# Four interleaved attention layers: a new table of slots, maxima that lead by 14 steps, accumulator copies on VectorE at a layer's end

## The chip, the cores and the metric

The kernel runs on one core of a Trainium2 chip. The metric is the time of one execution on the device, in microseconds; the kernel before is given as the median of three runs. A core has TensorE (PE, matrix products into eight PSUM banks of 128 x 512 fp32), VectorE (DVE), ScalarE (ACT), GpSimd (POOL) and SyncE (SP), which here issues all transfers. PE runs a weight load (PEld) and a matmul for each product.

## The reference, cut to what matters

Four layers run one after the other on x of 2048 rows and 576 columns, with 32 heads of 18 columns. Layers 0 and 2 ("A") have keys and values of their own for each head, layers 1 and 3 ("B") share one key and one value head.

```
x = x + _A_ref(_layernorm(x), A_wqkv, A_wo)
x = x + _B_ref(_layernorm(x), B_wq, B_wk, B_wv, B_wo)
x = x + _A_ref(_layernorm(x), A_wqkv, A_wo)
x = x + _B_ref(_layernorm(x), B_wq, B_wk, B_wv, B_wo)

scores = einsum("bhqd,bhkd->bhqk", q, k) * (Dh ** -0.5)
p = softmax(scores, axis=-1)
o = einsum("bhqk,bhkd->bhqd", p, v)
```

The softmax subtracts each row's maximum, so that the scores are computed twice: once for the maxima and once for the exponentials.

## The kernel before, in words

A layer has three parts: the projections (with the maxima of the first units woven between their matmuls), the attention, and the output projection. The order of every engine is the order in which the program is written; no scheduler moves anything, and each engine takes its instructions in that order.

**Units.** Two heads (a = 0, 1, a pair p) and 512 queries (u) make a unit; a layer has 64 units, w = 0 to 63. A unit needs 32 "e" products (L734: 64 rows by 512 queries; their exponentials are taken by ACT in L738 and written to `pt`), 32 tests for maxima and 4096 columns of "PV" (L759: the value product, 128 x 19 weights in four column groups, accumulated in the one bank `oacc`). Three kinds of product serve the maxima: "m" (L586, reduced by DVE in L593), "d" (L579, a difference of key blocks, of which ACT takes the positive part into `r`, L583) and "t" (an m whose reduction by DVE, L590, adds that `r`). Head a uses rows 64a to 64a+63 of PE, so that a pair of letters in the table below runs side by side.

**The table.** `UNIT` (L65) is the written order of a unit: each two-letter word is a pair, its first letter for head 0 and its second for head 1, and the number behind it is how many PV columns follow. Words up to a number are called a stretch here; the table has twelve. `LAST` (L67) is the table of the units that have no maxima left. PV lags the exponentials by `LAG` columns, and is cut where it passes a multiple of 512 columns, since a step's four `pt` tiles go together (`pv_cols`, L742). When a unit's PV is complete, `oacc` is copied to `oc` by ACT (L765), and the next PV may start only behind that copy.

**Maxima.** They lead the exponentials by `LEAD` steps; a unit has 8 steps of four e. With LEAD 16 the unit w of the table carries the maxima of unit w + 2, and the 32 pairs of maxima that come before the first unit are woven into the projections: `woven(max_pair, left, every)` (L273) puts one pair of m behind each `every` projection matmuls. `run_todo` (L833) issues at a given step what `at` has put down for it.

**Behind a unit's last maximum** DVE forms `neg` (L710), POOL splits it into `hl` (L713, L714), DVE transposes (L719), SP stores `m_d` (L721) and loads it back as two rows of the operand `big` (L725); the unit's exponentials need these rows. **Behind a unit's PV** POOL makes `os` out of `oc` (L772 by the helper line L179, then L773), SP loads `lt` (L778), POOL forms the reciprocal (L782), and so on to `o_d`.

**Buffers.** The e and d products share four PSUM banks (tag "e"), the m and t products have three (tag "m"); `oacc` is the eighth. The SBUF tiles `pt`, `r`, `oc` and those of the projections share 15 buffers (tag "p", L173): a new tile takes a buffer that is free in the written order, and its writer waits until the last reader of the old tile is done.

**Weights of the next layer** are loaded in the last units: `load(...)` puts a transfer into `raw`, and `finish_loads` (L212) splits what has arrived on POOL, which waits for the transfer there.

Of the kernel before, what the change touches and what calls it, by code (L numbers as in the profile page):

```python
# [10 lines left out]
AF = mybir.ActivationFunctionType  # L11
# [9 lines left out]
NPAIR = H // 2  # L21
# [21 lines left out]


STEPS = 8
LEAD = 16
NM_AT = 2
ROW_AT = 5
SUM_AT = 3
# [12 lines left out]

UNIT = """ee md 384 me me em 512 dm md em 320 me ee em 192 em me 384 et ee mm 384 me ee em 384 dm me em 384  # L65
          em me 256 me te ee 256 em em 384 et te me 256"""
LAST = "ee ee 512 " * 8  # L67
LAG = 896


def slots(text):
# [9 lines left out]
UNIT, LAST = slots(UNIT), slots(LAST)  # L81
# [4 lines left out]
def max_ops(kinds):  # L86
    pairs = kinds.count("d")
    rest = [(qc, kb) for qc in range(4) for kb in range(4) if qc >= pairs or kb > 1]
    seen, ops = {"d": 0, "t": 0}, []
    for k in kinds:  # L90
        if k == "m":
            ops.append((k, *rest.pop(0)))
        else:
            ops.append((k, seen[k], 0))
            seen[k] += 1
    assert not rest
    return ops


MAX_OPS = [max_ops(k) for k in KINDS]  # L100
PLAIN = [(i // 2 % 4, i // 8 % 2 * 2 + i % 2) for i in range(16)]
FIRST_SHARED = 3

# [2 lines left out]
def tile_kernel(ctx: ExitStack, tc: tile.TileContext, A_x, A_wqkv, A_wo, B_x, B_wq, B_wk, B_wv, B_wo, out):  # L106
    nc = tc.nc
# [67 lines left out]
    def copy(eng, dst, src):  # L175
        if eng is nc.scalar:
            eng.activation(dst, src, AF.Copy)
        else:
            eng.tensor_scalar(dst, src, 1.0, 0.0, op0=OP.mult, op1=OP.add)  # L179
# [93 lines left out]
    def woven(f, left, every):  # L273
        assert not weave["left"]
        weave.update(f=f, left=left, every=every, n=0)
# [119 lines left out]
    for layer in range(4):  # L395
# [159 lines left out]
        def max_mm(a, tile):  # L555

            n = m_next[a]
            w, i = divmod(n, 16)
            shared = w >= FIRST_SHARED
            kind = "m"  # L560
            if n < len(m_first):
                w, qc, kb = m_first[n]
            elif shared:
                kind, qc, kb = MAX_OPS[a][i]
            else:
                qc, kb = PLAIN[i]
            p, u = divmod(w, 4)
            q, k = ops(p)
            if (p, u) not in mxs:
                mxs[p, u] = mxd[w % 2] if shared else pool.tile([P, 32], F32, name="mx")  # L570
            mx = mxs[p, u]
            b = 64 * a
            c0 = u * 512 + qc * P
            r0 = 16 * a + 4 * qc + kb
            m_next[a] += 1
            m_done[0] += 1
            if kind == "d":
                ps = etile("psd")
                nc.tensor.matmul(ps, q[b:b + 3 * DH, c0:c0 + P], kds[p % 2 if is_a else 0][b:b + 3 * DH],  # L579
                                 start=True, stop=True)  # L580
                r = ptile("r")
                diffs[a].append(r)
                nc.scalar.activation(r, ps, AF.Relu)  # L583
            else:
                ps = tile("psm")
                nc.tensor.matmul(ps, q[b:b + KM, c0:c0 + P], k[b:b + KM, kb * 512:(kb + 1) * 512],  # L586
                                 start=True, stop=True)
                if kind == "t":
                    r = diffs[a].pop(0)
                    nc.vector.tensor_tensor_reduce(out=r, in0=ps, in1=r, scale=1.0, scalar=-3.0e38, op0=OP.add,  # L590
                                                   op1=OP.max, accum_out=mx[:, r0:r0 + 1])
                else:
                    nc.vector.reduce_max(mx[:, r0:r0 + 1], ps, axis=AX.X)  # L593
            m_count[p, u] = m_count.get((p, u), 0) + 1
            if m_count[p, u] == 32:
                max_final(p, u)

        def max_pair():
            if is_a and m_done[0] % 4 == 0:
                run_todo(m_done[0] // 4)  # L600
            for a in range(2):
                max_mm(a, etile if a else mtile)
            if not is_a and m_done[0] == 46:
                max_store(0, 0)
            elif not is_a and m_done[0] == 54:
                max_rows(0, 0)
# [53 lines left out]
        for T in range(4):  # L660
            if T == 0 and not is_a:
                fixed_rows(k_slot(0), True)
                fixed_rows(q_slot(0), False)
            if is_a:
                ts = range(0 if T or layer else 2, 9) if T < 3 else (6, 7, 8, 0, 4)
            else:
                ts = (4, 0, 1, 2, 3) if T < 3 else (4, 0, 1)
            for i, t in enumerate(ts):
                if not is_a and T == 2 and i == 1:
                    woven(max_pair, 12, 4)  # L670
                elif not is_a and T == 3:
                    woven(max_pair, *((3, 4), (4, 3), (4, 3))[i])
                project(T, t, not is_a and T >= 2)
                if is_a and T == 3 and i == 2:
                    load_k(0, 0, 1536)
                    load_q(0, 0, 512)
                    last_values()

                if T < 3 and (i % 2 != (T + layer == 0) if is_a else i < 4):
                    advance()  # L680
                if T == 0 and is_a and i < 6:
                    finish_loads(*((2,), (4,))[i] if layer == 0 and i < 2 else ())
                    if i < 4:
                        for c in (0, 1) if i == 0 else (i + 1,):
                            load_wsm(c, A_wqkv[:, 2 * D:])
                    if layer == 0 and i < 3:
                        load_x(5 + i)
                if not is_a and i < 2:
                    (load_q if i else load_k)(0, T * 512, T * 512 + 512)
                if vts and i != 0:  # L690
                    v_trans(*vts.pop())
            if is_a and T < 2:
                for c in range(4 * T, 4 * T + 4):
                    for h, ps in enumerate(project_v(c)):
                        nc.scalar.activation(v_dst(c)[:, h], ps, AF.Copy)
# [55 lines left out]
        def pv_block(n, c0, c1):  # L751

            p, u, i = *divmod(n // STEPS, 4), n % STEPS * 4
            cs = slice(c0, c1)
            turn[0] += 1
            for i in range(i, i + 4) if turn[0] % 2 else range(i + 3, i - 1, -1):
                a, kc = (i // 2) % 2, i // 4 * 2 + i % 2
                j = 64 * a + 32 * (kc % 2)
                nc.tensor.matmul(oacc[j:j + DH + 1, cs], v_of(kc)[:, 2 * p + a if is_a else 0, :], pts[p, u, i][:, cs],  # L759
                                 start=kc < 2 and c0 == 0, stop=kc >= 14 and c1 == 512)  # L760
                if c1 == 512:
                    pts.pop((p, u, i))
            if c1 == 512 and i // 4 == STEPS - 1:
                oc = ocs[p, u] = ptile("oc")
                nc.scalar.activation(oc, oacc, AF.Copy)  # L765


        def o_sum(p, u):
# [35 lines left out]
        def at(b, f, *args):  # L804
            todo.setdefault(b, []).append((f, args))
# [16 lines left out]
        for c in range(5):  # L822
            at(49 + 4 * c, finish_loads)
            at(48 + 4 * c, load_wsm, c, A_wo if is_a else B_wo, nc.gpsimd, nc.gpsimd, True)
            if layer < 3:
                b = LEAD + 32 * (NPAIR - 1) + 2 * c
                load = load_b if is_a else load_a
                at(b - 29, finish_loads)
                at(b + 3, finish_loads)
                at(b - 30, load, c, (2,), nc.gpsimd, nc.gpsimd, True)  # L830
                at(b + 2, load, c, (0,), nc.gpsimd, nc.gpsimd, True)

# [14 lines left out]
        late, n_e = LAG, 0  # L847
        for w in range(4 * NPAIR):
            p, u = divmod(w, 4)
            more_m = m_done[0] < 4 * ns  # L850
            e_next = [0, 0]
            for kinds, cols in UNIT if more_m else LAST:
                run_todo(LEAD + STEPS * w + sum(e_next) // 4)
                for a in range(2):
                    if kinds[a] == "e":
                        n = e_next[a]
                        e_next[a] += 1
                        exp_mm(p, u, n // 2 * 4 + 2 * a + n % 2, mtile if not more_m and n_e % 7 % 2 else etile)
                        n_e += 1
                    else:  # L860
                        max_mm(a, mtile)
                skip = min(late, cols)
                late -= skip
                pv_cols(cols - skip)
            assert e_next == [16, 16]
# [40 lines left out]
```

## Time and profile before

| | us |
|---|---|
| median of 3 runs (5727.47 to 5728.47) | 5728.04 |
| the profiled execution | 5728.76 |
| its span, first to last instruction | 5727.0 |
| PE busy | 5670.4 (99%) |
| DVE busy | 4936.5 (86%) |
| ACT busy | 4915.4 (86%) |
| POOL busy | 1744.0 (30%) |
| 16 DMA engines | 17.6% on the main queue |

The three large groups of PE are the m products (L586, 7216 matmuls), the e products (L734, 8192) and PV (L759, 30784 in the records, since each fp32 product of the program is two of them). ACT is mostly the 8192 exponentials of L738 (633 ns each, overlapping), DVE mostly the 6240 maxima of L593 (682 to 685 ns, overlapping). A row of the timeline is: start us, length us, engine, line, operation, output and inputs, form, count, and in brackets the engine's idle time ahead and what ended it. Ends of matmuls are modelled, so starts are what is read.

### The profile page before, as it was taken

What the parts mean: (1) busy time and instruction counts of PE and PEld (TensorE: products, weight loads), DVE (VectorE), ACT (ScalarE), POOL (GpSimd) and SP (SyncE); (2) the same over time, 40 slices, a digit from 0 to 9 for tenths busy, and PEclk for the clock granted to TensorE, in tenths of its full rate; (3) what the DMA queues carried; (4) which work ended last, traced back from release to release, by engine and by line L of the source; (5) the groups of instructions that cost most, each with busy time, mean ns of one, the idle gap of its engine ahead of it and who ended that gap; (6) DMA issues with size and microseconds to landing.
All of it is one profiled execution on the core that took longest, in us unless ns stands there. A gap on an engine that the chain in (4) does not pass through costs nothing.

```text
span 5727.0 us, 136567 instructions
## 1 busy us (share of the span) xinstructions
PE 5670.4 (99%) x51804; PEld 2876.1 (50%) x51804; DVE 4936.5 (86%) x9505; ACT 4915.4 (86%) x9876; POOL 1744.0 (30%) x2236
## 2 busy tenths in 40 slices
PE   9999999999999999999999999999999999999999
PEld 7644444444844444444585444444447444444446
DVE  4699999997689999999647999999976999999994
ACT  2499999999279999999725999999992899999995
POOL 3143333334123333333321333333332333333332
PEclk9999999999999999999999999999999999999999
DMA  6311111111320000100253111111113201010002
GB/s 227 107 48 36 39 35 38 39 35 27 123 65 23 24 23 20 24 23 24 60 187 95 49 38 35 39 38 36 37 39 120 58 23 23 20 24 23 20 17 78
DMA packets 258555, 291.48 MB, mean 51 GB/s; under 512 B 132700, under 2 KB 172892, under 8 KB 248176
## 3 DMA queue, kind: packets, MB, share of 16 engines
q1 hardware_dynamic: 257896, 282.75, 17.6%
q8 instruction: 407, 6.67, 0.5%
q14 instruction: 252, 2.06, 0.1%
HBM read 158.77 MB, written 119.86 MB: 49 GB/s over the span
## 4 chain that ended last, share of the span: by engine, by line
PE 96%; issue 1%; ACT 1%; POOL 1%; DMA 1%; DVE 1%; SPq 0%; ACTq 0%; POOLq 0%; DVEq 0%
PE oacc L759 37%; PE pse L734 22%; PE psm L586 20%; PE psn L257 6%; PE psq L414 6%; PE psd L579 4%; ACT pt L738 1%; PE ps L249 0%; POOL ev L429 0%; DVE mx L593 0%; DMA raw<-in_B_wk_dram 0%; DMA raw<-in_A_wqkv_dram 0%; DMA big<-qk_d 0%; SPq L191 0%; PE oacc L250 0%
## 5 line engine op out<-in xcount | busy, mean ns | idle before, releaser
L738 ACT ACTIVATE pt<-pse 128x512 f32<-128x512 f32 x8192 | 4202.5, 633 | 122.6 <-PE pse L734 53.2
L593 DVE TENSOR_REDUCE mxd<-psm 128x1 f32<-128x512 f32 x5856 | 3689.7, 682 | 115.9 <-PE psm L586 52.6
L586 PE MATMUL psm<-big 62*128 62x512 f32 x7216 | 2629.2, 450 | 10.3 <-DMA big<-qk_d 6.4
L734 PE MATMUL pse<-big 64*128 64x512 f32 x8192 | 2427.9, 439 | 1.8 <-ACT evr L428 1.6
L759 PE MATMUL oacc<-pt,vbuf 128*19 128x384 f32 (+5 forms) x23584 | 1789.0, 396 | 20.7 <-ACT oc L765 17.3
L734 PEld LDWEIGHTS pse<-big 64*128 64x128 f32 x8192 | 1231.5, 185 | 925.3 <-ACT pt L738 689.8
L586 PEld LDWEIGHTS psm<-big 62*128 62x128 f32 x7216 | 1188.9, 184 | 644.6 <-DVE mxd L593 255.8
L759 PEld LDWEIGHTS oacc<-pt,vbuf 128*19 128x19 f32 x23584 | 459.8, 97 | 687.6 <-issue 572.4
L590 DVE CUSTOM_DVE_ANT_0 r<-psm,r 128x512 f32<-128x512 f32 x976 | 652.7, 688 | 140.3 <-PE psm L586 118.3
L179 POOL TENSOR_SCALAR hl<-neg 128x8 fp32r<-128x8 f32 x256 | 50.6, 198 | 1813.6 <-DVE neg L710 1813.6
L759 PE MATMUL oacc<-pt,vy 128*19 128x128 f32 (+2 forms) x7200 | 593.4, 414 | 1.2
L583 ACT ACTIVATE r<-psd 128x512 f32<-128x512 f32 x976 | 581.8, 625 | 0.6 <-PE psd L579 0.6
L795 POOL TENSOR_TENSOR os<-os,rb 96x512 f32<-96x512 f32 x256 | 327.6, 1280 | 718.1 <-DMA rb<-r_d 714.3
L179 POOL TENSOR_SCALAR os<-oc 32x512 f32<-32x512 f32 x512 | 313.6, 612 | 676.1 <-issue 560.2
L782 POOL TENSOR_TENSOR rl<-lt,mone 128x8 f32<-128x8 f32 x256 | 422.2, 1649 | 97.5 <-DMA lt<-os 94.5
L579 PE MATMUL psd<-xx,big 54*128 54x512 f32 x976 | 402.9, 452 | 0.0
L422 ACT ACTIVATE ev<-psq 128x512 fp32r<-128x512 f32 (+1 forms) x112 | 66.9, 597 | 351.5 <-PE psq L414 278.8
L773 POOL TENSOR_TENSOR os<-os,oc 96x512 f32<-96x512 f32 x256 | 327.6, 1280 | 21.3
L257 PE MATMUL psn<-wsm,xx 128*128 128x288 f32 x2240 | 316.4, 298 | 2.1 <-ACT vy L497 2.0
L257 PEld LDWEIGHTS psn<-wsm,xx 128*128 128x128 f32 x2240 | 299.7, 188 | 21.0 <-issue 17.0
L593 DVE TENSOR_REDUCE mx<-psm 128x1 f32<-128x512 f32 x384 | 244.1, 685 | 56.6 <-PE psm L586 49.7
L579 PEld LDWEIGHTS psd<-xx,big 54*128 54x128 f32 x976 | 162.0, 184 | 258.5 <-ACT pt L738 207.2
(82 smaller groups left out, 2261.3 us busy)
## 6 DMA issues: line engine op xcount, KB each, us to landing
big<-qk_d SPq DMA_DIRECT2D x180, 432.0 KB
qk_d<-ev SPq DMA_DIRECT2D x96, 512.0 KB
qk_d<-ev SPq DMA_DIRECT2D x120, 256.0 KB
rb<-r_d SPq DMA_DIRECT2D x512, 36.0 KB
o_d<-os SPq DMA_DIRECT2D x512, 36.0 KB
m_d<-tr SPq DMA_DIRECT2D x1024, 2.0 KB
o<-o_d SPq DMA_DIRECT2D x64, 256.0 KB
big<-m_d SPq DMA_DIRECT2D x512, 4.0 KB
```

Source lines behind the costliest of these rows:

```text
L179: eng.tensor_scalar(dst, src, 1.0, 0.0, op0=OP.mult, op1=OP.add)
L257: nc.tensor.matmul(ps, lhs[:, xc, :], wsm[:, wc, h * 288:(h + 1) * 288], start=i == 0, stop=i == len(TERMS) - 1)
L414: nc.tensor.matmul(ps[:n].rearrange("p (u t) -> p u t", u=2)[:, us], w[:, wc, :n], xts[T][:, us, xc, :], start=(xc, wc) == TERMS[0], stop= ...
L579: nc.tensor.matmul(ps, q[b:b + 3 * DH, c0:c0 + P], kds[p % 2 if is_a else 0][b:b + 3 * DH], start=True, stop=True)
L583: nc.scalar.activation(r, ps, AF.Relu)
L586: nc.tensor.matmul(ps, q[b:b + KM, c0:c0 + P], k[b:b + KM, kb * 512:(kb + 1) * 512], start=True, stop=True)
L590: nc.vector.tensor_tensor_reduce(out=r, in0=ps, in1=r, scale=1.0, scalar=-3.0e38, op0=OP.add, op1=OP.max, accum_out=mx[:, r0:r0 + 1])
L593: nc.vector.reduce_max(mx[:, r0:r0 + 1], ps, axis=AX.X)
L734: nc.tensor.matmul(e, k[r:r + KE, kc * P:(kc + 1) * P], q[r:r + KE, u * 512:(u + 1) * 512], start=True, stop=True)
L738: nc.scalar.activation(pt, e, AF.Exp, scale=SCALE)
L759: nc.tensor.matmul(oacc[j:j + DH + 1, cs], v_of(kc)[:, 2 * p + a if is_a else 0, :], pts[p, u, i][:, cs], start=kc < 2 and c0 == 0, stop=k ...
L782: nc.gpsimd.tensor_tensor(rl, lts.pop((p, u)), mone, op=OP.pow)
```

## The change

- `LEAD` is 14: 28 pairs of maxima lie before the first unit in place of 32, and unit w of the table carries in its first eight words the last quarter of the maxima of unit w + 1, and behind them the first three quarters of unit w + 2 (`CUT`, `MAX_OPS`).
- `UNIT` is another order of the same counts: 32 e, 4 d, 4 t, 24 m and 4096 PV columns, in twelve stretches. `LAG` is 960.
- Unit 62, before a `LAST` unit, now takes `ENDS`: the first eight words of `UNIT`, then e alone. Unit 63 keeps `LAST`.
- `max_pair` takes an "e" bank for one maximum in four in place of one in two, and the weaving in the B layers is 10 pairs behind every 5 matmuls, 2 behind every 7, 4 behind every 3 twice (before: 12 behind every 4, 3 behind every 4, and the same two).
- Once a layer has no maxima left, `oc` is copied by DVE (units 61, 62 and 63).
- The splits of the next layer's weights stand two steps later, and one at a time.

```diff
-LEAD = 16
+LEAD = 14
...
-UNIT = """ee md 384 me me em 512 dm md em 320 me ee em 192 em me 384 et ee mm 384 me ee em 384 dm me em 384
-          em me 256 me te ee 256 em em 384 et te me 256"""
+UNIT = """md ee me 256 mm ee et 384 te em 320 me me ee 320 me em 384 em em md 448 ee em dt 448 me em em 384
+          em te 256 me em ee 384 mm de me 384 me em 128"""
 LAST = "ee ee 512 " * 8
-LAG = 896
+LAG = 960
+
+CUT = 4
...
-MAX_OPS = [max_ops(k) for k in KINDS]
+ENDS = UNIT[:8] + LAST[:10] + [["ee", 0], ["ee", 4096 - 5 * 512 - sum(n for _, n in UNIT[:8])]]
+assert [[w[a] for w, _ in UNIT[:8]].count("e") for a in range(2)] == [8 - CUT] * 2
+MAX_OPS = [max_ops(k[CUT:] + k[:CUT]) for k in KINDS]
...
             for a in range(2):
-                max_mm(a, etile if a else mtile)
+                max_mm(a, etile if m_done[0] % 4 == 3 else mtile)
...
                 if not is_a and T == 2 and i == 1:
-                    woven(max_pair, 12, 4)
+                    woven(max_pair, 10, 5)
                 elif not is_a and T == 3:
-                    woven(max_pair, *((3, 4), (4, 3), (4, 3))[i])
+                    woven(max_pair, *((2, 7), (4, 3), (4, 3))[i])
...
                 oc = ocs[p, u] = ptile("oc")
-                nc.scalar.activation(oc, oacc, AF.Copy)
+                copy(nc.scalar if m_done[0] < 4 * ns else nc.vector, oc, oacc)
...
-                at(b - 29, finish_loads)
-                at(b + 3, finish_loads)
+                at(b - 27, finish_loads, 1)
+                at(b + 5, finish_loads, 1)
...
-            more_m = m_done[0] < 4 * ns
+            more_m = w < 4 * NPAIR - 2
             e_next = [0, 0]
-            for kinds, cols in UNIT if more_m else LAST:
+            for kinds, cols in UNIT if more_m else ENDS if w == 4 * NPAIR - 2 else LAST:
...
-                        exp_mm(p, u, n // 2 * 4 + 2 * a + n % 2, mtile if not more_m and n_e % 7 % 2 else etile)
+                        exp_mm(p, u, n // 2 * 4 + 2 * a + n % 2, mtile if m_done[0] == 4 * ns and n_e % 7 % 2 else etile)
```

## The prediction

> **What bounds the kernel now.** I read the page first, then the busy time by stretches, then the timeline of one unit, since a unit repeats some 250 times.
>
> ```profile
> span 5727.0 us, 136567 instructions
> PE 5670.4 (99%) x51804; PEld 2876.1 (50%) x51804; DVE 4936.5 (86%) x9505; ACT 4915.4 (86%) x9876; POOL 1744.0 (30%) x2236
> ...
> L738 ACT ACTIVATE pt<-pse 128x512 f32<-128x512 f32 x8192 | 4202.5, 633 | 122.6 <-PE pse L734 53.2
> ```
> ```profile
> sum 378.00, PE 378.00 PEld 171.60 DVE 356.28 ACT 371.38 POOL 115.63; mean PE 18.90 PEld 8.58 DVE 17.81 ACT 18.57 POOL 5.78
> ```
> ```profile
> L765 ACT ACTIVATE oc<-oacc x43: 597/597/602, 404.9 to 1194.0; 128x512 f32<-128x512 f32 x43
> ```
>
> The second fence sums twenty stretches of 18.9 us from 400 us on: PE, ACT and DVE are all nearly full. The third holds one `oc` copy per unit: 42 units in 789.1 us, so a unit takes 18.79 us. A "busy" PE may be waiting, so its floor must be read from starts:
>
> ```profile
> 403.77 1.05 PE L759 MATMUL oacc<-pt,vy 128*19 128x512 f32 x8
> 404.76 0.50 PE L579 MATMUL psd<-xx,big 54*128 54x512 f32 x1
> ...
> 405.80 0.73 PE L759 MATMUL oacc<-pt,vbuf 128*19 128x320 f32 x8
> ...
> 410.30 0.85 PE L759 MATMUL oacc<-pt,vbuf 128*19 128x128 f32 x16
> 411.08 0.49 PE L586 MATMUL psm<-big 62*128 62x512 f32 x1
> ...
> 412.81 0.50 PE L579 MATMUL psd<-xx,big 54*128 54x512 f32 x1
> ...
> 413.71 0.84 PE L759 MATMUL oacc<-pt,vbuf 128*19 128x384 f32 x8
> ...
> 414.49 0.50 PE L734 MATMUL pse<-big 64*128 64x512 f32 x1
> ...
> 415.15 0.63 PE L759 MATMUL oacc<-pt,vy 128*19 128x256 f32 x8
> 415.71 0.49 PE L586 MATMUL psm<-big 62*128 62x512 f32 x1
> ```
>
> Three pairs take 0.90 us (412.81 to 413.71), two take 0.66 (414.49 to 415.15); 256 PV columns take 0.56 and 512 take 0.99, so 1.68 ns a column and 0.13 for the switch. Both tables have eight stretches of three pairs, four of two and 4096 columns: 7.20 + 2.64 + 12 x 0.13 + 6.88 = 18.28 us. The unit of before loses 18.79 - 18.28 = 0.51 us to waits; the worst is 404.76 to 405.80, 1.04 in place of 0.90. The change can gain that 0.51 at most in a unit, or lose more.
>
> **The change part by part: the table.** Its counts of e, d, m, t are those of before, so only waits can differ. I find four terms.
>
> (1) Small pieces. With `LAG` 960 PV starts a unit at column 64 of a block. Walking the table past the multiples of 512 gives five pieces of 64 columns: one each in the stretches of 448 (the second), 256 (the second) and 384 ("me em ee"), two in the last, of 128. Before, no piece is below 128.
>
> ```profile
> L759 PEld LDWEIGHTS oacc<-pt,vbuf x23584: 94/98/157, 233.8 to 5670.0; 128*19 128x19 f32 x200
> ```
>
> A piece is two rounds of four products side by side. A round of 128 columns streams 128 x 0.84 = 107 ns, just above the 98 ns that its four weights (loaded side by side during the round before) take; so the split of 384 into two pieces costs nothing (410.30 to 411.08, as 413.71 to 414.49). A round of 64 streams 54 ns and must wait for weights: about 109 ns from start to start. The 55 ns are lost seven times (a piece that ends a stretch loses one round, the one that begins a stretch two, the pair of 64 three): 0.39 us a unit. Bounds: 0 and ten rounds, 0.55. The Trainium skill ("TensorE: Matmul & The Clock Gate", LDWEIGHTS) gives a weight load as its columns over 1.2 ns, 16 ns for 19 columns; by it the pieces would cost nothing and the sum below would fall by 95 us. The trace disagrees: 94 is the shortest of 23584.
>
> (2) Banks. A product needs one of four e banks. An exponential starts 0.54 us behind its product's place in a stretch (0.00, 0.24, 0.47 for the three pairs; 0.50 of matmul), frees its bank 0.64 later (633 ns), and the next follows after 0.48. In "md ee me 256 | mm ee et" the first stretch puts four on an idle ACT: starts 0.54, 1.01, 1.49, 1.97. The third e of the next stretch needs the third's bank, free at 2.13, and its place is 0.90 + 0.56 + 0.47 = 1.93: 0.20 us lost. "me em 384" behind "me me ee" loses 0.03. Bounds of this term: 0, and 0.51, all that before loses. The maxima are spread more evenly than before (2 or 3 in each stretch, never 3 twice in a row, where before has 1, 3, 3), and the same walk finds no wait on DVE.
>
> (3) The buffer of `oc`.
>
> ```profile
> 402.51 0.19 DVE L710 TENSOR_REDUCE neg<-mxd 128x8 f32<-128x32 f32 x1
> ...
> 402.78 0.20 POOL L179 TENSOR_SCALAR hl<-neg 128x8 fp32r<-128x8 f32 x1 [6.41 <-DVE neg L710]
> ...
> 403.06 0.20 POOL L714 TENSOR_TENSOR hl<-neg,hl 128x8 fp32r<-128x8 f32 x1
> ...
> 404.90 0.60 ACT L765 ACTIVATE oc<-oacc 128x512 f32<-128x512 f32 x1
> ...
> 405.39 1.08 ACT L583 ACTIVATE r<-psd 128x512 f32<-128x512 f32 x2
> 405.64 1.30 POOL L179 TENSOR_SCALAR os<-oc 32x512 f32<-32x512 f32 x2 [2.38 <-issue]
> ...
> 406.34 7.37 ACT L738 ACTIVATE pt<-pse 128x512 f32<-128x512 f32 x14
> ...
> 407.02 1.28 POOL L773 TENSOR_TENSOR os<-os,oc 96x512 f32<-96x512 f32 x1
> ```
>
> POOL ends its sum 3.40 us behind the start of `oc` (408.30 - 404.90), and only then is `oc`'s buffer free. In the written order the ninth ACT operation behind `oc` takes that buffer before, two `r` and six `pt` ahead of it: it would start some 4.5 us behind `oc`, a margin of 1.1. That this wait binds when POOL is late, the trace shows once:
>
> ```profile
> 1312.15 1.26 POOL L773 TENSOR_TENSOR os<-os,oc 96x512 f32<-96x512 f32 x1
> ...
> 1313.45 2.07 ACT L738 ACTIVATE pt<-pse 128x512 f32<-128x512 f32 x4 [2.03 <-POOL os L773]
> 1314.10 0.14 PEld L759 LDWEIGHTS oacc<-pt,vbuf 128*19 128x19 f32 x8 [1.82 <-ACT pt L738]
> ```
>
> In the new order only six `pt` stand between, and the first e of "em em md 448" takes the buffer: 0.49 + 6 x 0.48 = 3.4 us behind `oc`, margin 0. And the last maximum of a unit now falls into the third stretch, whose PV ends the unit: counted from the table's start the four maxima and sums of stretches two and three occupy DVE from 2.01 to 5.22, `neg` ends at 5.4, when `oc` ends too. POOL's `hl` pair (0.56 from `neg`'s end to its own, 402.70 to 403.26), written first, holds the `os` copies back by 0.4. So ACT waits 0.3 to 0.5 us in each unit, all exponentials behind it queue, and the third and fourth e/d of "ee em dt" find their banks late: PE loses 0.2 to 0.4; I take 0.30. Bounds: 0 (POOL in time), and 0.5, all of ACT's wait.
>
> (4) `max_store`, `max_rows` come two steps later relative to the exponentials. The rows leave SP behind `lt`, which waits for POOL's sum: about 10 us into a unit of 19, so 8 us are left before they are read. I cost it at nothing; if a landing took over 8 us, each unit would wait for it.
>
> A unit so takes 18.28 + 0.39 + 0.23 + 0.30 = 19.20, 0.41 more than before; full units from the second to the 62nd are 61 in a layer, 244 in all: +100 us.
>
> **The ends of the layers.**
>
> ```profile
> 1400.26 1.08 PE L734 MATMUL pse<-big 64*128 64x512 f32 x4
> ...
> 1405.46 0.42 PE L759 MATMUL oacc<-pt,vbuf 128*19 128x128 f32 x8 [1.69 <-ACT oc L765]
> ...
> 1423.60 0.63 PE L759 MATMUL oacc<-pt,vbuf 128*19 128x128 f32 x8 [2.55 <-ACT oc L765]
> ```
> ```profile
> 1409.13 13.92 ACT L738 ACTIVATE pt<-pse 128x512 f32<-128x512 f32 x28 [0.73 <-PE pse L734]
> ...
> 1427.73 9.91 ACT L738 ACTIVATE pt<-pse 128x512 f32<-128x512 f32 x20 [0.68 <-PE pse L734]
> ```
>
> The last two units run from 1400.26 to the last exponential at 1437.64: 37.4 us. PE waits twice for `oc`, which stands behind up to seven exponentials in ACT's queue, and ACT starves after it. With DVE copying (it has no maxima left; some 0.6 us each, as on ACT) unit 62 takes three stretches (4.7 us with term 2) and then 56 exponentials at 0.49 (13.92 for 28): 0.5 + 4.7 + 27.4 = 32.6. That is -4.8 in this layer; I take -17 for four. If PE went on waiting for the copies, nothing would come.
>
> Four pairs fewer lie in each layer's projections:
>
> ```profile
> 184.80 0.93 PE L257 MATMUL psn<-wsm,xx 128*128 128x288 f32 x5
> 185.66 0.50 PE L586 MATMUL psm<-big 62*128 62x512 f32 x2
> 186.09 0.93 PE L257 MATMUL psn<-wsm,xx 128*128 128x288 f32 x5
> ```
> ```profile
> 1445.70 29.90 PE psn L257 x224
> ```
>
> A pair costs 1.29 - 5 x 0.133 = 0.63 us there (its maxima are covered by DVE at 1.25 a pair); sixteen are -10 us. They reappear in unit 62, already counted. In layers 1 and 3 the weaving puts the pair that needs the last keys some 5 us later:
>
> ```profile
> 1584.16 1.46 PE L586 MATMUL psm<-big 62*128 62x512 f32 x2 [3.11 <-DMA big<-qk_d]
> ```
> ```profile
> 1585.00:1590.00 5.00, 5.00 (x13) 2.69 (x14) 1.92 (x4) 1.09 (x2) 1.27 (x1) 0.50 0.29 108
> ```
>
> That wait of 3.1 us, and the half clock behind it (0.50), which stretches the next 7 us by some 3.4, go: -13 for both layers. Against it, the first maxima rows of a B layer now leave five pairs closer to the first exponential: 0 to 3 us each, +3 in all. The later splits remove what made POOL late at 1312, here and once in layer 2: -5. The e banks that `max_pair` leaves free and the longer run without PV in the first unit I cost at nothing, within 3 us a layer either way. Sum of the ends: -17 - 10 - 13 + 3 - 5 = -42 us (0 to -60).
>
> **Sum.** Against the profiled execution, 5728.76 (0.7 above the median shown): +100 - 42 gives 5787 us.
>
> **The rivals.** *POOL is in time* (the other side): if `neg` ends 0.4 us sooner than I find, term 3 is gone. A unit takes 18.90, +27 us; with the ends 5714, faster. It decides at POOL's sum ending within 3.4 us of `oc`'s start. For it: the margin without `hl` is 0; against it: a DVE which falls behind makes `neg` later, not sooner. *The pieces are free*: term 1 is gone, 244 x 0.39 = 95 us, 5692; against it the 98 ns. *More small waits*: before's unit loses 0.51, of which the two largest, 0.14 and 0.08, are what a walk of banks finds; if 0.25 of such waits lies on top here too, 5787 + 61 = 5848. *Both the first two*: 5787 - 73 - 95, about 5620.
>
> **How the numbers follow.** The forecast 0.50 (own range 5755 to 5820, by terms 2 and 3 and the ends), POOL in time 0.20, free pieces 0.08, more waits 0.20, both 0.02. The range 5700 to 5870 leaves out the free pieces and the tails, under 2 in 10. A measurement of this kernel can tell about 0.2% (11 us) from no change. Faster by more: 0.12 of the 0.20, 0.08 and 0.02, 0.22; within: 0.06; slower: 0.72.
>
> **What would show it.** The distance of `oc` copies in mid-layer: 19.2 us (18.9 if POOL is in time). ACT waiting for `os` L773 once in each unit, 0.3 to 0.5. PV pieces of 64 columns whose rounds start 109 ns apart. At a layer's end no wait of PE for `oc` above 1 us, and no half clock between 1400 and 1430. No wait of 3 us for `big` in layer 1. The prediction is wrong if units are below 18.8, or if a new wait that I cost at nothing, the maxima rows above all, binds in each unit.

## The result: 0.7% slower, and the profile after

| | before | after |
|---|---|---|
| median, us | 5727.76 (4 runs) | 5767.66 (5766.65 to 5769.43, 4 runs) |
| ratio, 95% interval | | 1.007 (1.0053 to 1.0088) |
| span of the profiled execution, us | 5727.0 | 5765.8 |

The forecast was 5787 us in a range of 5700 to 5870. The sum is near, but two of its terms are not: one price was wrong by nearly its whole size, and others made up for it. The page of the kernel after, its head and the row of the exponentials:

```profile
span 5765.8 us, 151755 instructions
...
PE 5733.0 (99%) x59516; PEld 3007.5 (52%) x59516; DVE 4918.9 (85%) x9517; ACT 4927.5 (85%) x9864; POOL 1741.8 (30%) x2236
...
L742 ACT ACTIVATE pt<-pse 128x512 f32<-128x512 f32 x8192 | 4252.7, 632 | 185.1 <-POOL os L777 99.9
```

The waits of ACT (us in total, times, longest), and the copies of `oc` from 404 to 1194 us (durations in ns, first and last start):

```profile
ACT pt L742 <- POOL os L777: 99.9, 240, 0.5
```
```profile
L181 ACT ACTIVATE oc<-oacc x42: 624/632/645, 404.6 to 1191.4; 128x512 f32<-128x512 f32 x42
```

ACT's idle time ahead of the exponentials has a new main releaser, POOL's sum `os`, in 240 units at 0.42 us each. Forty-one units take 1191.4 - 404.6 = 786.8 us, 19.19 each, against 18.79 before. One of these units, rows of its timeline from the copy of `oc` on (start, length, operation, and in brackets the idle time ahead and what ended it):

```profile
404.63 0.63 ACT L181 ACTIVATE oc<-oacc 128x512 f32<-128x512 f32 x1
...
405.08 0.19 DVE L714 TENSOR_REDUCE neg<-mxd 128x8 f32<-128x32 f32 x1
405.12 3.09 ACT L742 ACTIVATE pt<-pse 128x512 f32<-128x512 f32 x6
...
405.36 0.20 POOL L183 TENSOR_SCALAR hl<-neg 128x8 fp32r<-128x8 f32 x1 [10.89 <-DVE neg L714]
405.64 0.20 POOL L718 TENSOR_TENSOR hl<-neg,hl 128x8 fp32r<-128x8 f32 x1
405.93 1.30 POOL L183 TENSOR_SCALAR os<-oc 32x512 f32<-32x512 f32 x2
...
407.31 1.28 POOL L777 TENSOR_TENSOR os<-os,oc 96x512 f32<-96x512 f32 x1
...
408.63 1.08 ACT L742 ACTIVATE pt<-pse 128x512 f32<-128x512 f32 x2 [0.42 <-POOL os L777]
...
409.29 0.98 PE L738 MATMUL pse<-big 64*128 64x512 f32 x3
...
409.76 0.18 PEld L738 LDWEIGHTS pse<-big 64*128 64x128 f32 x1 [0.29 <-ACT pt L742]
...
410.25 0.18 PEld L583 LDWEIGHTS psd<-xx,big 54*128 54x128 f32 x1 [0.30 <-ACT r L587]
...
410.68 0.84 PE L763 MATMUL oacc<-pt,vbuf 128*19 128x384 f32 x8
```

Here is the third term in full: `neg` ends at 405.27, so `hl` ends only at 405.84, the copies start at 405.93 where `oc` had been ready since 405.26, the sum ends at 408.59, and the seventh exponential behind `oc` waits for it until 408.63. PE pays in the next stretch, "ee em dt": 410.68 - 409.29 = 1.39 us where three pairs need 0.90.

The end of the same unit and the first stretch of the next:

```profile
418.51 0.42 PE L763 MATMUL oacc<-pt,vy 128*19 128x64 f32 x16
418.86 0.50 PE L590 MATMUL psm<-big 62*128 62x512 f32 x1
...
419.59 0.18 PEld L738 LDWEIGHTS pse<-big 64*128 64x128 f32 x1 [0.20 <-ACT pt L742]
...
420.02 0.63 PE L763 MATMUL oacc<-pt,vy 128*19 128x256 f32 x8
```

The two pieces of 64 columns take 418.86 - 418.51 = 0.35 us from start to start. By the floor of the prediction, 0.13 + 128 x 1.68 ns, they need 0.345. The 0.165 us that the first term charged for this pair of pieces is not there. Instead "md ee me" takes 420.02 - 418.86 = 1.16, 0.26 above its floor, with a wait for an e bank.

Outside the units the span fell more than forecast. Its parts, from starts and ends in the two traces, in us, the four layers in order:

| part of a layer | before | after | difference, sum |
|---|---|---|---|
| first projection matmul to first e product | 217.9, 107.2, 205.1, 105.7 | 212.5, 93.7, 199.7, 93.8 | -36 |
| end of unit 60's copy to end of last exponential | 52.0, 53.1, 50.1, 52.0 | 46.9, 46.9, 47.0, 47.0 | -19.5 |

The second row holds unit 61, a full unit that is 0.41 longer (1.6 us in four layers), so the ends proper gave 21. With the late units of layers 0 and 2 (w = 57: 22.03 and 20.42 us before, 19.19 and 19.48 after), -5, and +1 in the first unit, this is -61 where the sum had -42. Units, 244 x 0.41 = +100, and the rest, -61, make the +38.8 between the spans.

### The profile page after: what moved, and what is told of

The parts are those of the page before. It is cut to its first block, busy times and chain, and to the rows that moved or that the text cites. A ratio compares the mean times of both kernels' runs of the same rounds, so it can differ in the third digit from the quotient of the medians.

```text
span 5765.8 us, 151755 instructions
## 1 busy us (share of the span) xinstructions
PE 5733.0 (99%) x59516; PEld 3007.5 (52%) x59516; DVE 4918.9 (85%) x9517; ACT 4927.5 (85%) x9864; POOL 1741.8 (30%) x2236
## 3 DMA queue, kind: packets, MB, share of 16 engines
q8 instruction: 467, 7.65, 0.5%
## 4 chain that ended last, share of the span: by engine, by line
PE 98%; DVE 1%; DMA 0%; ACT 0%; issue 0%; SPq 0%; POOL 0%; DVEq 0%; ACTq 0%; POOLq 0%
PE oacc L763 38%; PE psm L590 23%; PE pse L738 21%; PE psn L261 6%; PE psq L418 6%; PE psd L583 3%; DVE mx L597 0%; PE ps L253 0%; DMA raw<-in_A_wqkv_dram 0%; DMA qk_d<-ev 0%; PE oacc L254 0%; DVE oc L183 0%; DVE xx L247 0%; DVE ev L435 0%; DVE yx L247 0%
## 5 line engine op out<-in xcount | busy, mean ns | idle before, releaser
L742 ACT ACTIVATE pt<-pse 128x512 f32<-128x512 f32 x8192 | 4252.7, 632 | 185.1 <-POOL os L777 99.9
L590 PE MATMUL psm<-big 62*128 62x512 f32 x7216 | 2578.7, 454 | 6.8 <-DVE mx L597 5.5
L738 PE MATMUL pse<-big 64*128 64x512 f32 x8192 | 2486.7, 438 | 0.7 <-ACT evr L432 0.6
L763 PE MATMUL oacc<-pt,vbuf 128*19 128x320 f32 (+6 forms) x28368 | 1782.7, 355 | 6.8 <-DVE oc L183 6.7
L590 PEld LDWEIGHTS psm<-big 62*128 62x128 f32 x7216 | 1154.3, 184 | 851.5 <-DVE mxd L597 387.1
L763 PEld LDWEIGHTS oacc<-pt,vbuf 128*19 128x19 f32 x28368 | 581.8, 97 | 927.0 <-issue 723.9
L763 PE MATMUL oacc<-pt,vy 128*19 128x192 f32 (+4 forms) x10128 | 618.3, 342 | 0.0
L587 ACT ACTIVATE r<-psd 128x512 f32<-128x512 f32 x976 | 607.0, 622 | 0.1
L583 PE MATMUL psd<-xx,big 54*128 54x512 f32 x976 | 434.9, 446 | 0.0
L763 PEld LDWEIGHTS oacc<-pt,vy 128*19 128x19 f32 x10128 | 202.0, 97 | 259.3 <-issue 219.3
L597 DVE TENSOR_REDUCE mx<-psm 128x1 f32<-128x512 f32 x384 | 241.8, 684 | 36.4 <-PE psm L590 27.9
```

The lines of the kernel that those rows point to most:

```text
L738: nc.tensor.matmul(e, k[r:r + KE, kc * P:(kc + 1) * P], q[r:r + KE, u * 512:(u + 1) * 512], start=True, stop=True)
L742: nc.scalar.activation(pt, e, AF.Exp, scale=SCALE)
```

## The experiments

Each of them was timed beside the kernel before, whose medians there lay between 5725.2 and 5726.9 us.

**The buffer of `oc`.** `oc` gets two buffers of its own where weights do not need them:

```diff
-                oc = ocs[p, u] = ptile("oc")
+                own = 4 * p + u < 5 or 9 <= 4 * p + u < 56
+                oc = ocs[p, u] = pool.tile([P, 512], F32, tag="xh", bufs=2, name="oc") if own else ptile("oc")
```

> The changed kernel (5767.7 us), with `oc` in two buffers of its own in 52 of a layer's 64 units (the others, where weights pass through those buffers, stay as they are). Theory (the wait for `oc`'s buffer): ACT's wait for POOL's sum, 0.42 us in each unit, goes; the stretch "ee em dt 448", whose three pairs take 1.40 us from the first weight load to PV's first in place of 0.90, comes down to 0.90 to 0.95; a unit takes 18.69 in place of 19.19 and the run 5767.7 - 208 x 0.50 = 5664 us. Rival (the buffer costs PE the 0.30 of the prediction, the other 0.20 of that stretch being its own lack of banks): unit 18.9, run 5705. Rival (the wait only moves to the next late bank): 19.19, 5768.

Measured: 5663.7 us, ratio 0.9891 (0.9874 to 0.9907). The same rows of this kernel:

```profile
L181 ACT ACTIVATE oc<-oacc x42: 619/631/641, 421.5 to 1187.6; 128x512 f32<-128x512 f32 x42
```
```profile
421.47 0.63 ACT L181 ACTIVATE oc<-oacc 128x512 f32<-128x512 f32 x1
...
421.95 4.07 ACT L742 ACTIVATE pt<-pse 128x512 f32<-128x512 f32 x8
...
424.14 1.27 POOL L778 TENSOR_TENSOR os<-os,oc 96x512 f32<-96x512 f32 x1
...
426.12 0.73 PE L738 MATMUL pse<-big 64*128 64x512 f32 x3
...
427.03 0.84 PE L763 MATMUL oacc<-pt,vbuf 128*19 128x384 f32 x8
```

POOL's sum ends as late as in the changed kernel, 3.94 us behind the start of `oc`, but ACT runs through eight exponentials without a wait, and "ee em dt" takes 0.91. A unit takes 766.1 / 41 = 18.69. The units of the same execution that kept the shared buffers take 19.21, so the wait costs 0.5 us a unit, and that alone decides the sign of the whole change.

**`hl` on another engine.**

```diff
-            copy(nc.gpsimd, hl[:, 0:8], neg)
-            nc.gpsimd.tensor_tensor(hl[:, 8:16], neg, hl.bitcast(F32)[:, 0:8], op=OP.subtract)
+            copy(nc.vector, hl[:, 0:8], neg)
+            nc.vector.tensor_tensor(hl[:, 8:16], neg, hl.bitcast(F32)[:, 0:8], op=OP.subtract)
```

> The changed kernel with `hl` (L717, L718) made by VectorE in place of GpSimd, and all else kept, the 15 shared buffers too. Theory of the prediction (POOL's `hl` pair, written first, holds the copies of `oc` back by about half a microsecond, and without it POOL is just in time): the copies start some 0.14 us behind `oc`'s end, 0.5 sooner, ACT's wait of 0.42 us falls below 0.1, a unit takes 18.7 to 18.8 and the run 5655 to 5670 us. Rival (POOL is late by itself, or VectorE, which takes two operations more ahead of the next maxima, passes the delay on): the wait stays above 0.2 or new ones come, unit 18.95 to 19.2, 5705 to 5770 us.

Measured: 5791.6 us, ratio 1.0115 (1.01 to 1.013). Rows of one unit:

```profile
406.75 0.63 ACT L181 ACTIVATE oc<-oacc 128x512 f32<-128x512 f32 x1
...
407.18 0.19 DVE L714 TENSOR_REDUCE neg<-mxd 128x8 f32<-128x32 f32 x1
407.40 0.17 DVE L183 TENSOR_SCALAR hl<-neg 128x8 fp32r<-128x8 f32 x1
...
407.52 1.30 POOL L183 TENSOR_SCALAR os<-oc 32x512 f32<-32x512 f32 x2 [10.53 <-ACT oc L181]
407.61 0.55 DVE L718 TENSOR_TENSOR hl<-neg,hl 128x8 fp32r<-128x8 f32 x1
408.07 1.27 DVE L597 TENSOR_REDUCE mxd<-psm 128x1 f32<-128x512 f32 x2
...
410.60 1.08 ACT L742 ACTIVATE pt<-pse 128x512 f32<-128x512 f32 x2 [0.29 <-PE psm L590]
410.69 0.18 PEld L590 LDWEIGHTS psm<-big 62*128 62x128 f32 x1 [0.38 <-DVE mxd L597]
```

Half of each theory holds. The copies start 0.14 us behind `oc`, and ACT hardly waits for POOL's sum any more (0.8 us in the whole run, 99.9 in the changed kernel): the pair did hold them back. But from `neg` to the next maximum DVE now needs 0.89 us where it needed 0.11 (405.08 to 405.19), the maxima fall behind, and PE waits for their banks in "me em" and "em em md" (1.11 us each on the mean, 0.74 and 0.90 in the changed kernel). The unit came out at 19.3, longer than either theory had it: the price of a late engine was handed to another.

**Pieces of 64 columns.** Fewer of them, and nothing else but them:

```diff
-UNIT = """... ee em dt 448 me em em 384
-          em te 256 me em ee 384 mm de me 384 me em 128"""
+UNIT = """... ee em dt 384 me em em 384
+          em te 320 me em ee 320 mm de me 448 me em 128"""
```

> The changed kernel with other PV counts in four stretches (384, 320, 320, 448 in place of 448, 256, 384, 384 behind "ee em dt", "em te", "me em ee", "mm de me"), so that a unit has two PV pieces of 64 columns in place of five, and five pieces that end or begin inside a stretch in place of seven. Theory of the prediction (each round of 64 waits 55 ns for weights): four rounds fewer, -0.22 us a unit, 5767.7 - 54 = 5714 us. Rival (a piece costs only the 6 to 7 ns that the trace shows between one PV of 384 columns with and without a cut): -0.01 us a unit, and up to +0.1 where "mm de me 448" makes ACT idle; 5760 to 5790 us.

```diff
-                w = min(cols, 512 - c0)
+                w = min(cols, 512 - c0, 64)
```

> The changed kernel with every PV piece cut to at most 64 columns: 64 pieces a unit in place of 19, the same columns, twice and more the value products. Theory of the prediction (a round of 64 columns starts 109 ns behind the one before, for its weights): 128 rounds x 0.109 = 13.95 us of PV in place of 12 x 0.13 + 6.88 = 8.44, about +5 us a unit, +1200 us. Rival (the weights are loaded ahead, a piece costs 6 to 7 ns): 45 pieces more x 0.0065 = +0.3 us a unit, +75 us, some 5840 us.

Measured: 5784.8 us (ratio 1.0101, 1.0086 to 1.0116) with two such pieces in place of five, and 5815.7 us (1.016, 1.0144 to 1.0175) with nothing but such pieces. So fewer pieces gave nothing back (the larger stretch behind "mm de me" cost 0.11), and 45 more of them a unit cost 48 us, not 1200. The rows of the last kernel, its page's group, one stretch of 384 columns, and a place where PE stands still:

```profile
L763 PE MATMUL oacc<-pt,vbuf 128*19 128x64 f32 x98304 | 1833.6, 220 | 21.1 <-issue 14.4
```
```profile
419.52 0.87 PE L763 MATMUL oacc<-pt,vbuf 128*19 128x64 f32 x48
420.31 0.50 PE L738 MATMUL pse<-big 64*128 64x512 f32 x1
```
```profile
257.63 0.29 PE L763 MATMUL oacc<-pt,vbuf 128*19 128x64 f32 x4 [2.97 <-issue]
```

Forty-eight products are twelve rounds of four: (0.79 - 0.13) / 12 = 55 ns a round, the 54 that 64 columns stream. The weights of a round need not be loaded within the one round before it: their loads are recorded with 94 ns at least here too, and that is no bound on the distance of rounds. The Trainium skill ("TensorE: Matmul & The Clock Gate", the table of its head) says that PE pulls weight loads ahead of matmuls in flight; these runs agree.

From start to start the twelve PV of a unit take 8.67 us here and 8.44 in the changed kernel: 0.23 for 45 cuts, 5 ns each. The unit itself grows only from 19.19 to 19.30, because the stretches between wait less for banks ("ee em dt" takes 1.35 in place of 1.40). Longer regular units are so some 20 of the 48 us. Another 19 lie in fifteen single units, up to 4.5 us longer each; in the longest of them PE stands still for 2.97 us inside a PV, in the last row above, with nothing in the profile that it waits for. The page has 19.50 MB on the instruction queue in place of 7.65; whether such stops come from there was not tried.

**PV moved to where ACT is late.** The first experiment's kernel with other counts:

```diff
-UNIT = """md ee me 256 mm ee et 384 te em 320 me me ee 320 me em 384 em em md 448 ee em dt 448 me em em 384
-          em te 256 me em ee 384 mm de me 384 me em 128"""
+UNIT = """md ee me 320 mm ee et 320 te em 320 me me ee 384 me em 384 em em md 384 ee em dt 384 me em em 384
+          em te 256 me em ee 384 mm de me 384 me em 192"""
```

> As the first kernel (`oc` in buffers of its own), with other PV counts in the twelve stretches: 320, 320, 320, 384, 384, 384, 384, 384, 256, 384, 384, 192, chosen by the same walk of banks as in the prediction with pieces at no cost: the 64 columns more in each of the last and the first stretch let ACT catch up ahead of "md ee me" and "mm ee et". Theory (0.26 us of the first stretch is a wait for e banks that ACT frees): that stretch comes from 1.16 to 0.95 or less, a unit takes 18.45 to 18.5, the run 5600 to 5620 us, below both kernels. Rival (the first stretch waits for something else): no gain over the first kernel, 5664.

Measured: 5657.7 us (0.9879, 0.9865 to 0.9894). The first stretch fell only from 1.15 to 1.05 on the mean, "te em" and "me me ee" grew by 0.05 each, and a unit takes 18.67, 0.02 less. The theory of the bank holds for the place, not for the amount. The busy times of twenty such units offer a reason:

```profile
sum 373.34, PE 373.34 PEld 177.29 DVE 353.12 ACT 368.99 POOL 116.00; mean PE 18.67 PEld 8.86 DVE 17.66 ACT 18.45 POOL 5.80
```

ACT is busy for 18.45 of 18.67 us: it has hardly any time left to be given, so that PE's waits only move. No run with less work on ACT tested that.

**One buffer more.** The same counts, `oc` again in the shared buffers:

```diff
-        return pool.tile(list(shape), dt, tag="p", bufs=15, name=name)
+        return pool.tile(list(shape), dt, tag="p", bufs=16, name=name)
...
-    zeros = cst.tile([P, P], F32, name="zeros")
+    zeros = dram.tile([8, S], F32, name="zeros")
```

> The other counts of the fourth kernel, but `oc` in the shared buffers as in the changed kernel, with 16 of them in place of 15 in all units (constants of zeros and ones moved to DRAM make the room). Each tile then takes a buffer one exponential later, 0.48 us, where POOL was 0.42 us late. Theory (the wait is one of rotation, and the smallest cure is a buffer): it goes in every unit, those too that had no buffer of their own in the fourth kernel: 5657.7 - 48 x 0.50 = 5634 us, unit 18.66. Rival (POOL falls behind further once ACT does not wait): ACT still waits for the sum in most units, up to 0.3 us, 5660 to 5700 us.

Measured: 5652.7 us (0.9872, 0.9858 to 0.9887), the fastest of all. ACT's wait for the sum is gone (0.2 us in the whole run), which the theory asked for, but only 5 of its 24 us came. The full units without an own buffer had been eight in a layer, not twelve, which leaves 32 x 0.5 = 16 us to win; the units are 18.65 and 18.75 in turn, 0.04 longer on the mean than with buffers of their own (some 9 us, for a reason that was not found), and the constants in DRAM delay the start by 2.7.

**The ends of the layers.** In the changed kernel, ACT copies `oc` everywhere:

```diff
-                copy(nc.scalar if m_done[0] < 4 * ns else nc.vector, oc, oacc)
+                nc.scalar.activation(oc, oacc, AF.Copy)
```

> The changed kernel with ACT copying `oc` everywhere, as before, and all else kept. Theory (the copies behind ACT's exponentials held PE and so ACT at a layer's end): from the copy of unit 60 to the layer's last exponential, 46.95 us in each layer of the changed kernel and 50.1 to 53.2 before, 4 to 5 us come back in each layer, and PE waits for `oc` over 1.5 us; 5767.7 + 17 = 5785 us. Rival (the gain there is that of the table ENDS, which leaves the last 46 us with fewer switches between maxima and exponentials): under 1 us a layer, 5768 to 5771 us.

And the kernel before with VectorE's copies alone:

```diff
-                nc.scalar.activation(oc, oacc, AF.Copy)
+                copy(nc.scalar if m_done[0] < 4 * ns else nc.vector, oc, oacc)
```

> The kernel before with nothing but VectorE's copies of `oc` at a layer's end. Theory of the prediction (both of PE's waits there, 1.7 and 2.6 us, are for copies that stand behind exponentials in ACT's queue): both go, from the copy of unit 60 to the last exponential 50.1 to 53.2 us become 46 to 48.5, the run 5727 - 17 = 5710 us. Rival (the table ENDS does half of it, as the run with ACT's copies in the changed kernel suggests, where only one wait of 2.5 us and 2 us a layer came back): 49 to 51 us a layer, 5727 - 8 = 5719 us.

Measured: 5775.4 us (1.0086, 1.0071 to 1.0101) and 5710.3 us (0.9974, 0.9964 to 0.9984). PE's waits for `oc` in four layers, in the order before; before with VectorE's copies; after with ACT's; after:

```profile
PE oacc L759 <- ACT oc L765: 17.3, 8, 2.6
```
```profile
PE oacc L759 <- DVE oc L179: 8.3, 8, 1.3
```
```profile
PE oacc L763 <- ACT oc L769: 10.8, 8, 2.5
```
```profile
PE oacc L763 <- DVE oc L183: 6.7, 8, 0.9
```

Put into the kernel before, the copies bring unit 60's copy to last exponential down to 47.6, 47.6, 48.0 and 47.6 us, -16.6 in all: the prediction's -17, by its mechanism. Taken out of the kernel after, they cost only 7.6 there, since the table `ENDS` had already removed the shorter of the two waits. Without the copies the changed kernel so keeps some 13 us of its gain at the ends, the copies alone bring 16.6, and both together 21: the two take in part the same loss, and their gains do not add.

**The projections.** In the changed kernel, the woven maxima's banks as before, and then the weaving as before:

```diff
-                max_mm(a, etile if m_done[0] % 4 == 3 else mtile)
+                max_mm(a, etile if a else mtile)
```

> The changed kernel with the woven maxima's banks as before: head 1's always in an e bank. From a layer's first projection matmul to its first exponential product the change took 5.3, 13.5, 5.4 and 11.9 us off, 36 us, of which the prediction had 20. Theory 1 (the other banks are the rest: e banks taken by maxima hold up the woven exponentials and projections): 2 to 4 us a layer come back, 5767.7 + 12 = 5780 us. Theory 2 (a woven pair costs its whole 1.3 us, since the projections' own matmuls do not shrink beside it; four fewer are 5.2 us a layer): no change, 5768 us within 3.

```diff
-                    woven(max_pair, 10, 5)
+                    woven(max_pair, 12, 4)
...
-                    woven(max_pair, *((2, 7), (4, 3), (4, 3))[i])
+                    woven(max_pair, *((3, 4), (4, 3), (4, 3))[i])
```

> The changed kernel with the weaving of the B layers as before (12 pairs behind every 4 matmuls, 3 behind every 4, and the same two of 4 behind every 3), the 28 pairs in all kept. Theory (the new weaving took away a wait of 3.1 us for the last keys and the half clock behind it): both come back in layers 1 and 3, from the first projection to the first exponential product 93.8 us become 98 to 100.5 there, 5767.7 + 13 = 5781 us. Rival (with two steps less of lead the pair that needs the last keys stands elsewhere anyway; the gain is that of the fewer pairs): under 1 us a layer, 5768 to 5770 us.

And the kernel before with the new weaving alone:

> The kernel before with nothing but the new weaving in the B layers (10 pairs behind every 5 matmuls, 2 behind every 7; the other twelve of 32 pairs go into the fill behind). Theory formed from the traces (two gaps of PE in each B layer, 1.0 us for a bank behind DVE and 3.1 us for the last keys, each followed by 3 to 10 us of half clock, are what the new weaving takes away): from the first projection to the first exponential product 107.2 and 105.7 us become 94 to 97, the run 5727 - 23 = 5704 us. Theory of the prediction (only the wait for the keys and the half clock behind it): 5727 - 13 = 5714 us. Rival (it needs the shorter lead): no change, 5727 us.

Measured: 5770.6 us (1.0078, 1.0061 to 1.0095), 5795.2 us (1.0118, 1.0103 to 1.0133) and 5708.7 us (0.997, 0.9959 to 0.9981). The banks are worth some 3 us, most of it in layer 1. The old weaving in the changed kernel brings 108.5 and 105.5 us back in the B layers, +26.5, twice what its theory had; the new one in the kernel before gives 98.8 and 98.7, -15.4, between its two theories. The 5 us that are left in each B layer there go with what else the change does in this part. The traces offer 2.5 for four pairs fewer, 1.7 for 3.4 us at half clock that this run still has in each B layer, and 1.2 for shorter gaps of PE; no run took these one by one. What the weaving removes is seen in layer 1. PE's waits from the first projection to the first e product, before and then in the changed kernel with the old weaving:

```profile
PE psm L586 <- DMA big<-qk_d: 3.1, 1, 3.1
PE ps L249 <- DVE mx L593: 1.0, 1, 1.0
```
```profile
PE psm L590 <- DMA big<-qk_d: 3.4, 2, 3.2
PE psm L590 <- DVE mx L597: 1.5, 1, 1.5
```

And the busy times around the shorter of these waits, before (the stretch, its length, then PE, PEld, DVE, ACT and POOL with their counts; the third number from the right is the granted clock), and then the ten microseconds after that lie as far behind the layer's first projection, which starts 12.5 us later there:

```profile
1547.00:1549.00 2.00, 1.03 (x7) 0.58 (x6) 1.94 (x5) 1.08 (x2) 0.84 (x3) 1.00 0.80 170
...
1550.00:1560.00 10.00, 10.00 (x22) 5.07 (x22) 6.76 (x13) 0.73 (x4) 0.21 (x1) 0.50 0.25 90
```
```profile
1562.50:1572.50 10.00, 9.70 (x41) 5.67 (x40) 9.09 (x18) 1.75 (x4) 1.29 (x1) 1.00 0.44 159
```

PE stands still for one microsecond at 1547.8, for a bank behind DVE, and then runs at half the clock for ten: 22 matmuls, where the changed kernel runs 41. The prediction saw the wait of 3.1 us at 1581 and the seven slow microseconds behind it, but not this place, since the row of a wait of 1.0 us looks small.

## Why the prediction was right, and where not

- **Floor of the unit, 18.28.** Right. Stretches without a wait take 0.90, 0.666 and the PV time of the formula within 7 ns.
- **Term 1, small pieces, +0.39.** Wrong, and the step that failed is "a round of 64 streams 54 ns and must wait for weights: about 109 ns from start to start". Rounds start 55 ns apart. A cut costs 5 ns, at seven cuts 0.04 a unit. The step read a duration of a weight load as a bound on the distance of rounds, where the kernel before, with no piece below 128 columns, had no shorter round that could have shown it. The second rival, that the pieces are free, was true in its cause; by the rule of the Trainium skill ("TensorE: Matmul & The Clock Gate", LDWEIGHTS) the pieces cost nothing, which the runs bear out within 5 ns a cut, though the records' 94 ns are not its 16. "The trace disagrees" was too strong: the 94 ns are a length and not a distance. The sign that it named, pieces "whose rounds start 109 ns apart", is absent.
- **Term 2, banks, +0.23.** The mechanism is right, the size was 0.39 and the place another: 0.255 in "md ee me", 0.02 in "mm ee et", 0.07 in "me em 384", 0.045 in "mm de me". A likely reason for the place: with the last PV not lengthened by term 1, the first stretch comes sooner on ACT's backlog; it met the wait that the walk had put one stretch later.
- **Term 3, the buffer of `oc`, +0.30.** Right in each link: the late `neg`, the `hl` pair, POOL's sum, the first e of "em em md 448", ACT's wait (0.42, forecast 0.3 to 0.5), PE's loss in "ee em dt". Only the share that reaches PE was too small: 0.50, the upper bound of the prediction and a little more than ACT's wait. The stretch that it falls on holds three e and a d, and two of them wait for banks, 0.29 and 0.30 in the rows above; why nothing of it is caught up was not tried. The rival "POOL is in time" fell, and the run with the pair on DVE shows that its condition (`hl` out of the way) was the right one.
- **Term 4, the maxima's rows, 0.** Right: no instruction waits for `m_d` in the trace after.
- **Unit, 19.20.** It measured 19.19, because 0.35 too much in term 1 stood against 0.16 and 0.20 too little in terms 2 and 3. The number was right by compensation.
- **Ends, -42.** It was -61. The layer ends' -17 measured -21, the late splits' -5 came as forecast. What was mis-sized is the projections: -10 for the pairs and -13 for the wait for `big`, +3 for the rows, measured -36. In the B layers, -25.4 together, the step that was mis-sized is the wait of 3.1 us and the half clock behind it: it counted 6.2 us of waits and 6.8 lost at half clock. The trace before has 10.2 and 6.8 us at clock 0.50 in this part of layer 1, 3.4 and 10.2 in layer 3, and the trace after has none, which is worth up to 15.3; the gaps of PE fell by 7.6, and the pairs give 5: up to 27.9 for the 25.4 measured. The longer stretch of layer 3 before, and then this whole part of layer 1 after (PE stands still for 0.95 us of 93.6):

```profile
4430.80:4441.00 10.20, 9.16 (x21) 4.62 (x21) 4.14 (x7) 1.08 (x2) 1.27 (x1) 0.50 0.30 107
```
```profile
1512.40:1606.00 93.60, 92.65 (x415) 62.64 (x415) 72.09 (x146) 27.14 (x58) 21.63 (x33) 1.00 0.52 169
```

In the A layers, -10.7 together, the 2.5 us of four pairs in each are half, and waits of the projections before, which stand in no row of the trace after, are 3 us more (their rows before); the rest was not followed:

```profile
PE psn L257 <- ACT vy L497: 2.0, 4, 0.5
PE psq L414 <- ACT vy L497: 1.0, 2, 0.5
```

The mean granted clock of the two executions gives the size of what was overlooked:

```profile
core 0: 5727.0 us, clock 0.992
```
```profile
core 0: 5765.8 us, clock 0.998
```

0.006 of some 5746 us are 34 us of full clock, at most, since not all of it lay where PE was the bound. The forecast had counted 7 of them. Its signs at the ends came true: PE waits for `oc` 0.9 us at most, the half clock between 1400 and 1430 is gone, and so is the wait for `big` in layer 1.

## What to carry to other kernels

The length of an overlapped operation in the trace bounds nothing by itself: only a distance of starts does, and where the kernel before has no such distance, the price keeps both ends in the forecast. A tile that shares a rotating pool with many short-lived ones is freed by its slowest reader; count the writes of the order between it and the reuse of its buffer, and give it a buffer more before anything else is tuned (here 115 us of 5768, with the counts of PV, and both kernels beaten by 1.3 and 2.0%). And look for what short gaps of TensorE cost in the granted clock, not in the list of waits.

## What the runs showed of the hardware

A short gap on TensorE can cost more than its own length. Before, gaps of 0.97, 1.69, 2.55 and 3.11 us stand ahead of stretches at clock 0.50 that last about 3.4, 6.8 or 10.2 us, and others of up to 2.55 us ahead of none, so that one and the same gap at a layer's end is followed by half clock in layers 0, 1 and 3 and not in layer 2. Behind the gap of 0.97 us in layer 1 stand 10.2 us at half clock, so five us of work. In the kernel before with VectorE's copies the same gap is followed by ten microseconds at full clock, and the later wait for `big` by 17 us at half clock where it had 6.8; this part of layer 1 takes 107.6 us there and 107.2 before:

```profile
1545.17 0.66 PE L249 MATMUL ps<-ident,xh 128*128 128x128 f32 x4 [0.97 <-DVE mx L593]
```
```profile
1550.00:1560.00 10.00, 9.90 (x45) 5.74 (x43) 9.07 (x16) 2.81 (x7) 1.29 (x1) 1.00 0.28 101
...
1576.40:1593.40 17.00, 16.36 (x37) 8.57 (x38) 7.82 (x15) 2.17 (x4) 2.95 (x4) 0.50 0.19 67
```

So the amount of half clock in this part was much the same, and not the gap behind which it came. The Trainium skill ("TensorE: Matmul & The Clock Gate", Part 1) tells of a free-running window of about 3.4 us; the lengths agree with multiples of it. It also has the clock fall behind a whole idle window, and warns of gaps above 3.4 us; here half clock followed a gap of 0.97 us, and the measurement decides. What share of a window must be idle, and how much the lighter work around a gap adds, these runs do not settle.
